# A scheduler that knows how long things take: traced durations, overlaps and a hold on TensorE in a four-layer transformer kernel

## The chip, the cores and the metric

The kernel runs on one core of a Trainium2 chip. The metric is the time of the whole kernel on the device, in microseconds, from the first to the last instruction of that core. A core has five engines that run their own instruction streams and wait for each other through semaphores: TensorE (PE; its weight loads are listed as PEld) for matrix products, VectorE (DVE), ScalarE (ACT), GpSimd (POOL), and SyncE (SP), which issues transfers here.

## The reference

Four layers over x of 2048 tokens by 512: attention, feed-forward, attention, feed-forward, with the same weights for both attentions and for both feed-forwards. Each has a layer norm before it and adds to x; the feed-forward has a second layer norm of its own.

```python
def _A_ref(x, wqkv, wo):                  # attention, 32 heads of 16
    qkv = (x @ wqkv) ...                  # q, k, v: (1, 32, 2048, 16)
    scores = jnp.einsum("bhqd,bhkd->bhqk", q, k) * scale
    p = _softmax(scores, axis=-1)
    o = jnp.einsum("bhqk,bhkd->bhqd", p, v)
    return o... @ wo
def _B_ref(x, w1, b1, w2, b2):            # feed-forward, 1376 wide
    y = _layernorm(x, axis=-1)
    h = _gelu(jnp.einsum("bsd,df->bsf", y, w1) + b1)
    return jnp.einsum("bsf,fd->bsd", h, w2) + b2

x = A_x
x = x + _A_ref(_layernorm(x, axis=-1), A_wqkv, A_wo)
x = x + _B_ref(_layernorm(x, axis=-1), B_w1, B_b1, B_w2, B_b2)
x = x + _A_ref(_layernorm(x, axis=-1), A_wqkv, A_wo)
x = x + _B_ref(_layernorm(x, axis=-1), B_w1, B_b1, B_w2, B_b2)
```

With 32 heads of 16, each attention has 32 x 2048 x 2048 scores, so exponentials[...]. Cut into tiles of 128 keys by 512 queries that is 4096 tiles for both attentions.

## The kernel before

The kernel is a Python program that works like a list scheduler. It keeps a model of the five engines: when each is free (`free`), when each value was written (`t1`) and read. Jobs hand in tasks with a priority (lower goes first), a modelled duration, and what they read and write. The scheduler picks the task that can start earliest, appends its instructions to its engine's stream, and moves the model's clock on. What the chip gets is only the order on each engine and the semaphores; the modelled times are not in it. But they decide the order, and some decisions on the work itself.

The model: an operation starts when its engine is free and what it depends on is ready.

```python
LAT_SAME = 0.07
LAT_CROSS = 0.13
LAT_PE = 0.22
PE_SWITCH = 0.107          # TensorE changes its tiling
...
    def ready(self, eng, reads, writes, same_ok=()):
        ...                # d: an operation that this one depends on
                x = d.t1 + (LAT_SAME if d.eng == eng else LAT_PE if d.eng == "pe" else LAT_CROSS)
        ...
        return t
    def op(self, eng, fn, reads=(), writes=(), same_ok=(), dur=0.3, lat=None):
        op.t0 = max(self.free[eng], self.ready(eng, reads, writes, same_ok))
        ...
        elif eng == "pe":
            how, tile = lat or ("full", 0)
            if how != self.tiling:
                op.t0 = max(op.t0, self.drain + PE_SWITCH)
            ...
        else:
            op.t1 = op.t0 + dur
            self.free[eng] = op.t1
```

The choice on an engine: of the tasks that are ready when it is free, the one with the lowest priority number; if none is ready, the one that will be ready first.

```python
    def best(self, e):
        f = self.P.free[e]
        lim = f + self.LOOK[e]
        for t in lst:
            r = self.task_ready(t)
            if r <= lim:
                k = (t.prio, t.seq)
                if bk is None or k < bk:
                    b, bk = t, k
                    br = r
            else:
                ...        # late: the one that will be ready first
```

The work of attention. TensorE makes scores for 3 and 2 tiles in turn (PSUM banks 0 to 2 and 3 to 4); ScalarE takes the exponential of a group in one instruction:

```python
            yield Task("pe", 0.0, ops)                                        # L1204: scores
            S_.submit(Task("act", 1e-5 * gi, [I(lambda e, ...: e.activation(
                out=self.PT[:, pt:pt + n, :], in_=self.ps[:, b0:b0 + n, :],
                func=ACTF.Exp, scale=EXPS), ..., 0.089 + 0.4267 * n)]), ...)  # L1189
```

A tile of certain key blocks can go to VectorE instead. There the bits of the exponential are made by an addition with rounding to 16-bit integers (L1281), then three shifted copies (L1312), which together with four scaled versions of V approximate the exponential. Such a tile needs four products with V (L1373) in place of one. Whether a tile goes there is decided by the model:

```python
    def take_d(self, hps):
        if ... self.dload > 1 or P.free["dve"] - S_.now > 1.3 \
               or sum(o[4] for t in S_.pend["dve"] for o in t.ops) > DBACK:   # 2.0
            return None
        ...                # up to 4 - (tiles of the group) are attached to each group of scores
    # L1281                                                        modelled 0.66
    e.tensor_scalar(out=self.dp[...], in0=self.ps[:, b, :], scalar1=BITS0, ..., op0=ALU.add)
    # L1312, N = 1024 for two tiles, three times                   modelled 0.1 + 0.26e-3 * N
    e.tensor_scalar(out=self.dp[:, v, 0:N], in0=self.dp[:, u, 0:N], scalar1=float(SHIFT[k]), ..., op0=ALU.add)
```

The scores have priority 0.0 and an attached VectorE tile's scores -0.5. A VectorE tile that is scored on its own has 0.5, a product of probabilities with V 1.0, and output projection, feed-forward and the next layer's q, k and v have 0.95 to 2.2. While TensorE has a gap of over 0.2 us in the model, `fill_pe` puts products into it whose result nobody uses (L1114, L1117)[...]. GELU (L1530, L1531) runs on ScalarE between the exponentials and needs two table loads each time.

Of the kernel before, what the change touches and what calls it, by code (L numbers as in the profile page):

```python
# [13 lines left out]
ACTF = mybir.ActivationFunctionType  # L14
ALU = mybir.AluOpType
# [4 lines left out]
LAT_SAME = 0.07  # L20
LAT_CROSS = 0.13
LAT_PE = 0.22
# [40 lines left out]
class Prog:  # L63
# [14 lines left out]
    def ready(self, eng, reads, writes, same_ok=()):  # L78
        t = 0.0
        lw, rd = self.last_writer, self.readers  # L80
        for r in reads:
            d = lw.get(r)
            if d is not None and not (d.eng == eng and r in same_ok):
                x = d.t1 + (LAT_SAME if d.eng == eng else LAT_PE if d.eng == "pe" else LAT_CROSS)
                if x > t:
                    t = x
        for w in writes:
            d = lw.get(w)
            if d is not None and not (d.eng == eng and w in same_ok):
                x = d.t1 + (LAT_SAME if d.eng == eng else LAT_PE if d.eng == "pe" else LAT_CROSS)  # L90
                if x > t:
                    t = x
            q = rd.get(w)
            if q:
                for d in q.values():
                    if not (d.eng == eng and w in same_ok):
                        x = d.t1 + (LAT_SAME if d.eng == eng else LAT_PE if d.eng == "pe" else LAT_CROSS)
                        if x > t:
                            t = x
        return t  # L100

    def op(self, eng, fn, reads=(), writes=(), same_ok=(), dur=0.3, lat=None):
# [10 lines left out]
        if eng == "sp":  # L113
            self.free[eng] = op.t0 + dur
            op.t1 = op.t0 + dur + (2.0 if lat is None else lat)
# [4 lines that stand above are left out]
                self.tiling, self.tiles = how, {}  # L120
            op.t0 = max(op.t0, self.tiles.get(tile, 0.0))
            op.t1 = op.t0 + dur
            self.tiles[tile] = op.t1
            self.drain = max(self.drain, op.t1)
            self.work.append((op.t0, op.t1, 1.0 if how == "full" else 0.25))
            self.free[eng] = op.t0 + min(dur, PE_ISSUE)
        else:
            op.t1 = op.t0 + dur
            self.free[eng] = op.t1
# [134 lines left out]
class Sched:  # L264
# [44 lines left out]
    def _step(self, gen, prio, val):  # L309
        while True:  # L310
# [24 lines left out]
            if kind == "ready":  # L335
                r = self.P.ready(req[1], req[2], ()) - 0.3
                if r <= self.now:
                    continue
                self.seq += 1
                heapq.heappush(self.timers, (r, self.seq, lambda: self._step(gen, prio, None)))  # L340
                return
# [31 lines left out]
    def best(self, e):  # L373
        lst = self.pend[e]
        if not lst:
# [3 lines that stand above are left out]
        b = None  # L379
        bk = None  # L380
        late = None
        lk = None
        for t in lst:
            r = self.task_ready(t)
            if r <= lim:
                k = (t.prio, t.seq)
                if bk is None or k < bk:
                    b, bk = t, k
                    br = r
            else:  # L390
                k = (r, t.prio, t.seq)
                if lk is None or k < lk:
                    late, lk = t, k
        if b is not None:
            return (max(f, br), b)
        return (lk[0], late)

# [28 lines left out]

FILL_GAP = 0.2
# [24 lines left out]
class Builder:  # L452
# [314 lines left out]
    def ln_group(self, tiles, slot, prio, eps1, eps0):  # L767

        for i, tt in enumerate(tiles):
            c = 4 * slot + i  # L770
            s = yield ("get", "st")
            yield Task("dve", prio, [I(lambda e, s=s, tt=tt: e.bn_stats(out=self.st[:, s, :], in_=self.xres[:, tt, :]), [("x", tt)], [("st", s)], 0.65)])
            yield Task("dve", prio, [I(lambda e, s=s, c=c: e.bn_aggr(out=self.mv[:, c, :], in_=self.st[:, s, :]), [("st", s)], [("mv", c)], 0.18)])
            self.S_.release("st", s)
# [5 lines left out]
        yield Task("pool", prio, [I(lambda e: e.tensor_scalar(out=rs, in0=var, scalar1=eps1, scalar2=eps0, op0=ALU.mult, op1=ALU.add), [("mv", c0 + i) for i in range(n)], [R], 0.25)])  # L780
        yield Task("pool", prio, [I(lambda e: e.tensor_tensor(out=rs, in0=rs, in1=self.cneg[:, 0:n], op=ALU.pow), [R, ("cneg",)], [R], 0.45 + 0.1 * n)])

    def ln_apply(self, tt, slot, i, dst, dres, prio):
        c = 4 * slot + i
        return Task("dve", prio, [I(lambda e: e.tensor_scalar(out=dst, in0=self.xres[:, tt, :], scalar1=self.mv[:, c, 0:1], scalar2=self.rs[:, c:c + 1], op0=ALU.subtract, op1=ALU.mult),
                                    [("x", tt), ("mv", c), ("rs", slot)], [dres], 0.39)])
# [19 lines left out]
    def job_qkv_tile(self, L, tt, slot, i, left, prio, what):  # L806
# [74 lines left out]
        yield Task(eng, prio, [I(lambda e: e.tensor_tensor(out=sq, in0=v4, in1=v4, op=ALU.mult), [("qk", qs, k) for k in range(k0, k1)], SR, 0.12 + 0.0085 * N if eng == "dve" else 1.15)])  # L881
# [26 lines left out]
    def bound_rows(self, qs, ns, RN, prio, eng="pool"):  # L908
# [7 lines left out]
        yield Task(eng, prio, [I(lambda e: e.tensor_tensor(out=a, in0=x, in1=y, op=ALU.mult), RN + [("qy", ns)], [RA], 0.35 if eng == "pool" else 0.17)])  # L916
        yield Task(eng, prio, [I(lambda e: e.tensor_tensor(out=c, in0=a, in1=y, op=ALU.mult), [RA, ("qy", ns)], [RC], 0.3 if eng == "pool" else 0.17)])
        yield Task(eng, prio, [I(lambda e: e.tensor_scalar(out=c, in0=c, scalar1=-0.5, scalar2=1.5, op0=ALU.mult, op1=ALU.add), [RC], [RC], 0.28 if eng == "pool" else 0.17)])
        yield Task(eng, prio, [I(lambda e: e.tensor_tensor(out=a, in0=a, in1=c, op=ALU.mult), [RA, RC], [RA], 0.3 if eng == "pool" else 0.17)])
        yield Task(eng, prio, [I(lambda e: e.tensor_scalar(out=pads(self.qks(qs)[:, 0, :])[:, :, 16:17], in0=a.rearrange("p (n o) -> p n o", o=1), scalar1=-MARG, scalar2=0.0, op0=ALU.mult, op1=ALU.add),  # L920
                                    [RA], [QQ], 0.4 if eng == "pool" else 0.17)])
# [120 lines left out]
    def job_qt(self, sg, s):  # L1042
# [8 lines left out]
                                  [RS, ("scl", k), ("qbias",)], [("qt", q)], 0.39)])  # L1051
# [8 lines left out]
    def job_vs(self, sg, i, kbs):  # L1060
# [5 lines left out]
                                   [("V", hg, kb) for kb in kbs], [("vs", q, i + k2) for k2 in range(n)], 0.27 + 0.167 * n, [("vs", q, i + k2) for k2 in range(n)] if k > 1 else []) for k in (1, 2, 3)])  # L1066
# [58 lines left out]
    def flow_scores(self):  # L1125
# [11 lines left out]
        while True:  # L1137
# [45 lines left out]
            if len(ops[0]) > 1:  # L1183
# [6 lines left out]
                                                [("ps", b) for b in banks], [("pt", pt + k) for k in range(n)], 0.089 + 0.4267 * n)]),  # L1190
# [86 lines left out]
    def d_load(self, d):  # L1277
# [4 lines left out]
                                           [("ps", b)], [("dp", u, w)] + self.dres(u), 0.66)]),  # L1282
# [21 lines left out]
    def job_d(self, bt):  # L1304
# [4 lines left out]
        for k in range(1, len(SHIFT)):  # L1309
# [3 lines left out]
                                     [("dp", u, w) for w in range(n)], [("dp", v, w) for w in range(n)] + self.dres(v), 0.1 + 0.26e-3 * N)])  # L1313
# [82 lines left out]
    def job_segend(self, sg):  # L1396
# [6 lines left out]
        yield Task("dve", 0.3, [I(lambda e: e.transpose(self.accT[:, a, 0:W], self.ps[:, ACCB, 0:W]), [("ps", ACCB)], [RA], 0.15 + 0.53 * W / 512)])  # L1403
# [21 lines left out]
        if nparts == 2:  # L1425
# [4 lines left out]
            yield Task("act", -1.0, [I(lambda e: e.activation(out=dw, in_=dw, func=ACTF.Exp, scale=EXPS), [RW], [RW], 0.2)])  # L1430
            yield Task("pool", 1.2, [I(lambda e: e.tensor_tensor(out=M, in0=M, in1=dw.unsqueeze(2).broadcast_to([128, 16, 16]), op=ALU.mult), [RW, RO], [RO], 0.75),
                                     I(lambda e: e.tensor_tensor(out=den, in0=den, in1=dw, op=ALU.mult), [RW, RD], [RD], 0.2),
                                     I(lambda e: e.tensor_tensor(out=T[:, :, 16], in0=T[:, :, 16], in1=den, op=ALU.add), [RD, RA], [RA], 0.2),
# [7 lines left out]
        yield Task("dve", 1.2, [I(lambda e: e.tensor_tensor(out=ob[:, :, 0:16], in0=T[:, :, 0:16], in1=rv.unsqueeze(2).broadcast_to([128, nb, 16]), op=ALU.mult), [RA, ("rv", a)], [("ob", o)], 0.15 + 0.26 * W / 512)])  # L1441
# [66 lines left out]
    def job_ffn(self, L, qc):  # L1508
# [8 lines left out]
        for fc in range(NFC):  # L1517
# [7 lines left out]
                                               [("ps", b), ("b1c",)], self.hres(fc * W // 512), 0.1 + 0.52 * W / 512, [("h", fc * W // 1024)])]),  # L1525
# [4 lines left out]
        yield Task("act", -1.0, [I(lambda e: e.activation(out=self.gv[:, 0:nf * W], in_=hv[:, 0:nf * W], func=ACTF.Gelu_apprx_tanh), HR, HR, 1.5 + 0.427 * nf * W / 512),  # L1530
                                I(lambda e: e.activation(out=self.g10[0:self.FLAST, 0:W], in_=hv[0:self.FLAST, nf * W:(nf + 1) * W], func=ACTF.Gelu_apprx_tanh), HR, [("g10",)], 0.5 + 1.3)])  # L1531
# [23 lines left out]
    def job_tail(self, L, qc):  # L1555
# [14 lines left out]
        yield Task("act", pr, [I(lambda e: e.activation(out=self.kmx[:, 2:3], in_=self.kmx[:, 0:1], func=ACTF.Gelu_apprx_tanh), [("kmx", 0)], [("kmx", 2)], 1.4)])  # L1570
# [14 lines left out]
        for fc in range(NFC):  # L1585
# [5 lines left out]
                                          [("ps", b), ("b1c",)], [("gt", fc)] + (HR if fc == 0 else [("g10",)] if fc == nf else []), 0.16 + 0.52 * W / 512)]),  # L1591
# [122 lines left out]
```

## Time and profile before

| | before |
|---|---|
| median of 3 runs | 1661.06 us (1657.99 to 1662.54) |
| span of the profiled run | 1661.8 us |
| busy: PE, DVE, ACT | 1608.0, 1452.7, 1582.4 us |
| score tiles through ScalarE, through VectorE | 3270, 826 |
| mean granted TensorE clock | 0.994 of full |

The profile's groups name a line of the kernel, an engine, an operation, what it writes and reads with its shape, how often it ran, its total and mean duration, and the idle time of the engine before it with what ended most of that. The waits name who waited, for whom, how long in total, how often, and the longest. Durations of two consecutive instructions on ScalarE or VectorE can overlap, so a busy share is one thing, and how often an instruction can start another. On the time line each row is an instruction or a merged run of the same kind: start, length, engine, line, and in brackets the idle time before it and who ended it.

### The profile page before, as it was taken

To read this page: it belongs to the slowest core of one execution; us is meant where nothing else is said; L and a number is where in the kernel's file an instruction comes from. 1 tells how busy PE (TensorE), PEld (TensorE's weight loads), DVE (VectorE), ACT (ScalarE), POOL (GpSimd) and SP (SyncE) were. 2 spreads that over 40 slices of the span, in tenths; PEclk is the share of its full clock that TensorE was granted. 3 is DMA by queue.
4 is the path that set the end of the run, shared out by engine and by line. 5 is a ranking of instruction groups with operands and counts; after the bars stand their busy time and mean duration, and the time that the engine had idled before them with its cause. 6 is when DMAs were issued, how large, how long until landed. Compare 5 with 4: busy or idle time off the path is not lost.

```text
span 1661.8 us, 42068 instructions
## 1 busy us (share of the span) xinstructions
PE 1608.0 (97%) x17575; PEld 529.0 (32%) x17575; DVE 1452.7 (87%) x3146; ACT 1582.4 (95%) x1400; POOL 376.1 (23%) x575
## 2 busy tenths in 40 slices
PE   8999999999999999999999999999999999999998
PEld 5223322222222232222232323322232232344444
DVE  7789998888899898998989789999898969899893
ACT  4899999999999999999999999999999999999996
POOL 4345331111210112111121125511111111232220
PEclk9999999999999999999999999999999999899999
DMA  6562100202111121102362321000000000000000
GB/s 170 103 125 62 27 8 8 42 19 61 56 23 42 26 52 53 33 26 58 95 94 57 59 64 42 18 18 8 20 5 11 17 16 5 5 9 20 22 7 14
DMA packets 181243, 66.43 MB, mean 40 GB/s; under 512 B 160859, under 2 KB 175424, under 8 KB 181056
## 3 DMA queue, kind: packets, MB, share of 16 engines
q1 hardware_dynamic: 181056, 63.75, 17.3%
q8 instruction: 141, 2.31, 0.6%
q14 instruction: 46, 0.38, 0.1%
HBM read 19.96 MB, written 15.30 MB: 21 GB/s over the span
## 4 chain that ended last, share of the span: by engine, by line
PE 65%; ACT 27%; DVE 6%; issue 1%; DMA 1%; POOL 0%; POOLq 0%; SPq 0%; DVEq 0%
ACT PT L1189 25%; PE ps L1204 24%; PE ps L1373 19%; PE ps L840 5%; PE ps L1500 4%; PE ps L1538 4%; PE ps L1114 4%; PE ps L1467 3%; DVE dp L1281 2%; DVE dp L1312 2%; ACT h L1530 1%; PE ps L1117 1%; PE ps L953 1%; DMA xnT<-xn 0%; ACT L1189 0%
## 5 line engine op out<-in xcount | busy, mean ns | idle before, releaser
L1189 ACT ACTIVATE PT<-ps 128x1024 bf16<-128x1024 f32 (+1 forms) x1321 | 1506.4, 1259 | 49.5 <-PE ps L1204 43.1
L1204 PE MATMUL ps<-QT,KT 32*128 32x512 bf16 (+1 forms) x4608 | 681.8, 359 | 39.0 <-ACT PT L1189 16.9
L1281 DVE TENSOR_SCALAR dp<-ps 128x512 uint16<-128x512 f32 x826 | 558.2, 684 | 117.0 <-PE ps L1204 108.0
L1312 DVE TENSOR_SCALAR dp<-dp 128x1024 uint16<-128x1024 uint16 (+1 forms) x1257 | 488.8, 431 | 11.1 <-PE ps L1373 6.7
L1373 PE MATMUL ps<-PT,V 128*17 128x512 bf16 (+1 forms) x3672 | 486.7, 360 | 0.3 <-ACT PT L1189 0.3
L1065 POOL TENSOR_SCALAR vs<-V 128x340 bf16<-128x340 bf16 (+3 forms) x240 | 238.5, 995 | 875.3 <-PE ps L1373 851.0
L1373 PE MATMUL ps<-dp,vs 128*17 128x512 bf16 (+1 forms) x2808 | 420.7, 357 | 0.0
L1204 PEld LDWEIGHTS ps<-QT,KT 32*128 32x128 bf16 x4608 | 176.4, 91 | 568.3 <-issue 170.7
L1373 PE MATMUL ps<-dp,V 128*17 128x512 bf16 (+1 forms) x936 | 204.6, 359 | 2.7 <-DVE accT L1403 2.5
L1114 PE MATMUL ps<-wqkv,zw 128*32 128x256 bf16 x3792 | 182.0, 277 | 0.4 <-DVE dp L1281 0.4
L1373 PEld LDWEIGHTS ps<-PT,V 128*17 128x17 bf16 x3672 | 116.4, 88 | 119.4 <-issue 107.5
L1373 PEld LDWEIGHTS ps<-dp,vs 128*17 128x17 bf16 x2808 | 106.2, 89 | 113.6 <-issue 94.2
L1114 PEld LDWEIGHTS ps<-wqkv,zw 128*32 128x32 bf16 x3792 | 97.1, 96 | 67.1 <-issue 50.0
L1500 PE MATMUL ps<-yT,wf 128*128 128x512 bf16 (+3 forms) x396 | 101.7, 360 | 0.3 <-DVE dp L1281 0.3
L840 PE MATMUL ps<-wqkv,xnT 128*128 128x512 bf16 x336 | 96.1, 389 | 4.3 <-DMA xnT<-xn 3.4
L1403 DVE STREAM_TRANSPOSE accT<-ps 128x512 f32<-128x512 f32 (+1 forms) x88 | 58.0, 659 | 13.7 <-PE ps L1373 12.7
L1467 PE MATMUL ps<-wo,OT 128*128 128x512 bf16 x240 | 67.2, 383 | 0.0
L1373 PEld LDWEIGHTS ps<-dp,V 128*17 128x17 bf16 x936 | 50.5, 89 | 48.1 <-issue 26.7
L1524 DVE TENSOR_SCALAR h<-ps,b1c 128x512 bf16<-128x512 f32 (+2 forms) x88 | 61.9, 704 | 3.6 <-PE ps L1500 2.9
L1443 DVE STREAM_TRANSPOSE OT<-ob 128x512 bf16<-128x512 bf16 (+1 forms) x72 | 46.0, 638 | 0.2
L1500 PEld LDWEIGHTS ps<-yT,wf 128*128 128x128 bf16 (+1 forms) x396 | 28.1, 99 | 54.2 <-issue 26.9
L1538 PE MATMUL ps<-wf,h 128*128 128x512 bf16 x160 | 44.9, 383 | 0.1
(171 smaller groups left out, 794.7 us busy)
## 6 DMA issues: line engine op xcount, KB each, us to landing
wf<-in_B_w_dram SPq DMA_DIRECT2D x90, 128.0 KB, 2.6
q_scr<-qk SPq DMA_DIRECT2D x22, 256.0 KB, 2.0
k_scr<-qk SPq DMA_DIRECT2D x12, 256.0 KB, 2.1
out_dram<-xres SPq DMA_DIRECT2D x16, 128.0 KB, 1.7
v_scr<-vst SPq DMA_DIRECT2D x12, 136.0 KB, 1.7
V<-v_scr SPq DMA_DIRECT2D x8, 204.0 KB, 4.7
wqkv<-in_A_wqkv_dram SPq DMA_DIRECT2D x3, 512.0 KB, 3.9
q_scr<-h SPq DMA_DIRECT2D x6, 256.0 KB, 3.6
```

Source lines behind the costliest of these rows:

```text
L840: yield Task("pe", prio, [I(lambda e, c=c: e.matmul(self.ps[:, b, :], lhsT=xnT[:, c, :], rhs=self.wqkv[:, c, which * 512:which * 512 + 512 ...
L1065: yield Task("pool", 0.8, [I(lambda e, k=k: e.tensor_scalar(out=self.vs[:, q, k - 1, i:i + n, :], in0=src, scalar1=WSHIFT[k], scalar2=None ...
L1114: P.op("pe", lambda e, p=p: e.matmul(self.ps[p:p + 32, b, 0:w], lhsT=self.zw[:, 0:32], rhs=rhs[:, 0:w], start=st, stop=st, skip_group_chec ...
L1189: S_.submit(Task("act", 1e-5 * gi, [I(lambda e, pt=pt, n=n, b0=b0: e.activation(out=self.PT[:, pt:pt + n, :], in_=self.ps[:, b0:b0 + n, :] ...
L1204: return [I(lambda e, kb=kb, i=i: e.matmul(self.ps[:, b, i * W:(i + 1) * W], lhsT=self.KT[32 * hp:32 * hp + 32, hg, kb * 128:(kb + 1) * 12 ...
L1281: self.S_.submit(Task("dve", 0.0, [I(lambda e: e.tensor_scalar(out=self.dp[:, u, w * 512:(w + 1) * 512], in0=self.ps[:, b, :], scalar1=BIT ...
L1312: yield Task("dve", pr, [I(lambda e, k=k, v=v: e.tensor_scalar(out=self.dp[:, v, 0:N], in0=self.dp[:, u, 0:N], scalar1=float(SHIFT[k]), sc ...
L1373: ops.append((i, I(lambda e, hp=hp, v=v, ap=ap[:, i * W:(i + 1) * W], first=first and i == 0, W=W: e.matmul(self.ps[32 * hp:32 * hp + 17, ...
L1467: yield Task("pe", pr, [I(lambda e, hg=hg, i=i, b=b: e.matmul(self.ps[:, b, :], lhsT=self.OT[:, hg, i * 128:(i + 1) * 128], rhs=self.wo[:, ...
L1500: yield Task("pe", pr, [I(lambda e, c=c: e.matmul(self.ps[0:M, b, off:off + W], lhsT=self.w1(fc, c), rhs=self.yT[:, c, 0:W], start=(c == 0 ...
L1524: S_.submit(Task("dve", pr - 0.7, [I(lambda e, fc=fc, M=M, b=b: e.tensor_scalar(out=hv[0:M, fc * W:(fc + 1) * W], in0=self.ps[0:M, b, 0:W] ...
L1538: yield Task("pe", pr, [I(lambda e, fc=fc, i=i, b=b: e.matmul(self.ps[:, b, :], lhsT=self.gt(fc, i, W), rhs=self.w2(L, fc), start=(fc == 0 ...
```

## The change

The scheduler's model gets the durations that a trace of the kernel shows, in place of rounder ones; it lets an instruction on ScalarE, VectorE or GpSimd start before the one ahead of it has ended, by a fixed overlap; and the delay from a dependency to the start now belongs to the engine that waits, with an extra for results of TensorE. Beside that comes a rule for TensorE: a task with priority over 0 (products with V, projections, feed-forward, a VectorE tile on its own) is passed over if the next scores will be ready within 1 us and TensorE would drain too late for them. The purpose is that the order fits the engines as they are, and that ScalarE doesn't wait for scores. The computation is the same.

```diff
-LAT_SAME = 0.07
-LAT_CROSS = 0.13
-LAT_PE = 0.22
+LATENCY = {"act": 0.036, "dve": 0.036, "pool": 0.086, "pe": 0.057, "sp": 0.06}
+LAT_PE = 0.174
+OVERLAP = {"act": 0.127, "dve": 0.08, "pool": 0.05}
 PE_SWITCH = 0.107
...
-                x = d.t1 + (LAT_SAME if d.eng == eng else LAT_PE if d.eng == "pe" else LAT_CROSS)
+                x = d.t1 + LAT_PE if d.eng == "pe" else d.t1
...
-        return t
+        return t + LATENCY[eng] if t else 0.0
...
             op.t1 = op.t0 + dur
-            self.free[eng] = op.t1
+            self.free[eng] = op.t0 + (max(0.02, dur - OVERLAP[eng]) if lat is None else lat)
...
+        due = self.scores_due(f, lim) if e == "pe" else None
         for t in lst:
             r = self.task_ready(t)
             if r <= lim:
+                if due is not None and t.prio > 0.0 and self.drained(t, max(f, r)) + PE_SWITCH > due:
+                    continue
...
+    def scores_due(self, f, lim):
+        first = None
+        for t in self.pend["pe"]:
+            if t.prio == 0.0:
+                r = self.task_ready(t)
+                if r > lim and (first is None or r < first):
+                    first = r
+        if first is None or first - f > HOLD_REACH:
+            return None
+        act = self.P.free["act"] + sum(max(0.02, o[4] - OVERLAP["act"]) for t in self.pend["act"] for o in t.ops)
+        return max(first, act - HOLD_LEAD) + HOLD_LATE
+
+    def drained(self, task, t):
+        ...                # when TensorE would have done this task, its tiling switch included
...
+HOLD_REACH = 1.0
+HOLD_LEAD = 0.45
+HOLD_LATE = 0.4
...                        # exponential of n tiles, L1189
- ... 0.089 + 0.4267 * n)]),
+ ... 0.174 + 0.428 * n)]),
...                        # VectorE's tiles, L1281 and L1312
- ... 0.66)]),
+ ... 0.682)]),
- ... 0.1 + 0.26e-3 * N)])
+ ... 0.151 + 0.2605e-3 * N)])
...                        # bias before GELU, L1524
- ... 0.1 + 0.52 * W / 512, ...
+ ... 0.2 + 0.54 * W / 512, ...
...                        # GELU, L1530 and L1531: durations, and when ScalarE is free again
- ... 1.5 + 0.427 * nf * W / 512), ... 0.5 + 1.3)])
+ ... 1.5 + 0.427 * nf * W / 512, (), 1.313 + 0.2 + 0.427 * nf * W / 512), ... 0.2 + 0.427 * W / 512, (), 0.2 + 1.32 + 0.427 * W / 512)])
```

Some twenty more durations of small operations (layer norms, norms of queries and keys, scaled copies of V, transposes) change in the same way, most by 0.01 to 0.1 us.

## The prediction

> **What bounds the kernel now.** I read the page's busy times first, then the groups by form, then who waits for whom, then the time line round one wait.
>
> ```profile
> PE 1608.0 (97%) x17575; PEld 529.0 (32%) x17575; DVE 1452.7 (87%) x3146; ACT 1582.4 (95%) x1400; POOL 376.1 (23%) x575
> ```
>
> Three engines look full. ScalarE (ACT) is the one that is: TensorE (PE) holds filler products among its 1608 us, and a busy PE is not PE at its peak. The groups by form:
>
> ```profile
> L1189 ACT ACTIVATE PT<-ps 128x1536 bf16<-128x1536 f32 x628 | 931.0, 1483 | 29.6 <-PE ps L1204 23.7
> L1189 ACT ACTIVATE PT<-ps 128x1024 bf16<-128x1024 f32 x693 | 727.5, 1057 | 19.9 <-PE ps L1204 19.3
> ...
> L1281 DVE TENSOR_SCALAR dp<-ps 128x512 uint16<-128x512 f32 x826 | 558.2, 684 | 117.0 <-PE ps L1204 108.0
> L1312 DVE TENSOR_SCALAR dp<-dp 128x1024 uint16<-128x1024 uint16 x1221 | 479.8, 434 | 11.0 <-PE ps L1373 6.7 <-DVE xres L1469 0.3
> ...
> L1114 PE MATMUL ps<-wqkv,zw 128*32 128x256 bf16 x3792 | 182.0, 277 | 0.4 <-DVE dp L1281 0.4
> ```
>
> The 4096 score tiles of 512 columns are split: 628 x 3 + 693 x 2 = 3270 go through ScalarE's exponential, 826 through VectorE (one read from PSUM, and three shifted copies for each pair of tiles). So each tile that moves from ScalarE to VectorE shortens ScalarE's queue. L1114 is filler. The waits:
>
> ```profile
> DVE dp L1281 <- PE ps L1204: 108.0, 210, 3.5
> ...
> PEld ps L1204 <- ACT PT L1189: 62.1, 165, 0.9
> ...
> ACT PT L1189 <- PE ps L1204: 43.1, 102, 4.1
> ```
>
> ScalarE waits for scores 43.1 us in 102 places, VectorE 108 us. One such place on the time line:
>
> ```profile
> 277.48 0.60 PE L1204 MATMUL ps<-QT,KT 32*128 32x512 bf16 x3
> 278.01 0.55 PEld L1467 LDWEIGHTS ps<-wo,OT 128*128 128x128 bf16 x4 [0.42 <-issue]
> 278.02 1.04 PE L1467 MATMUL ps<-wo,OT 128*128 128x512 bf16 x4
> 278.12 0.69 DVE L1281 TENSOR_SCALAR dp<-ps 128x512 uint16<-128x512 f32 x1 [0.20 <-PE ps L1204]
> 278.98 0.11 PEld L1204 LDWEIGHTS ps<-QT,KT 32*128 32x128 bf16 x4 [0.42 <-PE ps L1467]
> 278.99 0.60 PE L1204 MATMUL ps<-QT,KT 32*128 32x512 bf16 x4
> 279.48 1.45 ACT L1189 ACTIVATE PT<-ps 128x1536 bf16<-128x1536 f32 x1 [0.27 <-PE ps L1204]
> ```
>
> Four output-projection products went between two sets of scores; the second set came late and ScalarE stood 0.27 us. This is what the hold is aimed at.
>
> **What the Trainium skill says.** "ScalarE: Activation LUTs", under "What ACT_TABLE_LOAD costs", gives an ACTIVATE with immediate operands 186 ns + 0.833 ns per element, and says that neighbours overlap by about 93 ns. The trace agrees in form: means of 1483 and 1057 ns (the rule gives 1466 and 1039), and consecutive starts lie a median 1.331 us apart after a 3-tile exponential and 0.903 (lower quartile) after a 2-tile one, so they overlap by some 0.10 to 0.13. "TensorEngine Tiling (Array Packing)", under "Key Properties", says that changing the tiling mode drains TensorE: above, the scores of 277.48 start 0.53 us after the first of two full products (276.95), which stream for 0.43, so a switch costs about 0.10, as the kernel's constant (0.107, unchanged) has it. "VectorE: DVE Perf Modes", under "Why PSUM operands drop a tier", explains why L1281 takes 684 ns for 512 elements from PSUM, while L1312 takes 434 for 1024 in SBUF. "TensorE: Matmul & The Clock Gate", under "What's actually happening", says that an idle array falls to half clock: this trace has a mean of 0.994, and 0.86 in 1400 to 1450 us.
>
> **The change, part by part.** No instruction gets another shape; the order on each engine, and the split between ScalarE and VectorE, come out of the model, and the model changes.
>
> 1. *ScalarE's durations.* Old model: 0.089 + 0.4267n, so 1.369 and 0.942 for n = 3 and 2: 2.311 us for five tiles. New: 0.174 + 0.428n - 0.127, so 1.331 and 0.903: 2.234. The trace has 1.331 + 0.903 = 2.234. The old order was laid out for a ScalarE 3.4% slower than it is, so TensorE took on other products in time that wasn't there. The whole floor: 628 x 1.331 + 693 x 0.903 = 1462 us, or 0.447 per tile; the remaining 199 us are GELU with its table loads (about 60), start and tail (28 us before the first exponential, 22 after the last), and gaps. Adding up how much each start is late against 1.331 or 0.903 gives 88 us from first to last exponential, some 80 of it in gaps over 0.1 us, a gap being here a delay with or without a named wait.
>
> 2. *VectorE's durations.* Old: 0.66 for L1281, 0.1 + 0.26 x 1.024 = 0.366 for L1312; a pair of tiles costs 2 x 0.66 + 3 x 0.366 = 2.42 us. New: 0.682 - 0.08 = 0.602 and 0.151 + 0.267 - 0.08 = 0.338; a pair costs 2.22. The trace has medians of 0.608 and 0.336 between starts: 2.22. So VectorE gets 8% cheaper in the model, ScalarE only 3.4%. Tiles are given to VectorE as long as its modelled backlog is under 1.3 us (and 2.0 us pending), so it should get more of them. How many? Old model: 826 tiles x 1.21 + about 490 for other work = 1490, which is 90% of 1661. New: 1.10 per tile; other work is 461 us (546 measured less 0.08 for each of 1063). If the model again fills 90%: 1.10n + 461 = 0.9T, with T = 1641 - 0.447(n - 826) (20 us of gaps already gone): n = 896. If instead only the measured share is kept (durations less 0.08: 499 + 441 + 461 = 1401 us, 84%): n = 835. I take the middle, **865**: 39 tiles x 0.447 = **-17 us** on ScalarE. The pending limit still adds up full durations, which grew, and the hold keeps PSUM readers waiting; hence not the upper end.
>
> 3. *The hold.* Products with priority over 0 wait when they would drain later than the next scores are due plus 0.4 us. That forbids the long delays (277 to 279 above), not those of 0.2 us. With part 1 I let 20 to 25 of the 80 us go: **-20 us**. The first 60 us (14 us of score waits while the first keys arrive) are DMA and product latency, and stay.
>
> 4. *What it costs.* Each tile moved to VectorE needs four products with V instead of one: 39 x 3 x 0.216 / 4 = 6 us of TensorE, off the path as long as there is filler to give up. From 100 to 1640 us the starts on TensorE divide into 590 us of scores, 483 of products with V, 301 of full products, 165 of filler and the gaps before what follows it. So 165 us are spare, and a time 37 us shorter takes them to about 120. Enough on average, not in each stretch.
>
> Sum: 1661 - 17 - 20 = **1624 us**.
>
> **Rivals.** *TensorE becomes the bound.* Holding makes it stand idle, and what is held (feed-forward, projections, next layer's keys) comes due at the layer's end near 850 to 960 us, where ScalarE already loses 6.7 us. For it: 97% busy, and only a tenth spare. Against: that tenth is filler. Then the hold's gain is given back: about 1645 to 1660. *VectorE takes many more tiles.* For it: 108 us of waits for scores and the 90% estimate above; against: L1281 waits for TensorE, which serves it together with ScalarE's scores. Then 890 to 900 tiles, 30 us, and with the gaps: 1600 to 1610. *Only the model changes, the chip hardly follows.* ScalarE is 95% busy and every order that keeps it fed is nearly as good; the limits tuned to the old model (1.3, 2.0, 0.3 ahead) fit the new one less well: 1640 to 1660. *More half clock.* Held stretches could let the array idle: a stretch like 1400 to 1450, with 3.9 us of waits, costs some 4 us each time.
>
> **Range and chances.** The good end is part 2's upper count with 35 us of gaps recovered: 1661 - 31 - 35 = 1595, so 1592 to be safe. The bad end is no gain with a little noise: 1656. 2% faster is 1627.8, just above the sum, so it is little better than even: faster 0.54, same 0.41, slower 0.05, the last for a jam on TensorE that the spare 165 us don't cover.
>
> **What would show it.** Right: L1281 rises from 826 to about 865 and L1189's tiles fall from 3270 to about 3230; ACT's wait for L1204 falls from 43 to about 25, DVE's from 108 to under 90; filler L1114 falls from 3792 to near 2800; L1189's share of the chain rises over 25%. Wrong in part 2: L1281 stays within 10 of 826. Wrong in part 3: ACT's wait for L1204 stays over 38, or PE's waits on ACT grow by as much as ACT's fall. The whole is wrong if ScalarE's busy share falls under 94%.

## The result, and the profile after

| | before | after |
|---|---|---|
| median | 1660.42 us (4 runs, 1657.99 to 1662.54) | 1641.84 us (4 runs, 1640.56 to 1643.21) |
| ratio, 95% interval | | 0.9887 (0.9871 to 0.9903) |
| tiles through ScalarE, VectorE | 3270, 826 | 3227, 869 |
| ScalarE's wait for scores | 43.1 us | 43.0 us |
| filler products L1114, now L1150 | 3792 | 2928 |

The change takes 18.6 us off, 1.1%. In the changed file attention and feed-forward stand 36 lines lower: L1240 makes the scores, L1225 is the exponential, L1317 and L1348 are VectorE's tiles, L1409 the products with V, L1566 GELU. The page's busy times:

```profile
PE 1555.6 (95%) x16682; PEld 504.4 (31%) x16833; DVE 1481.7 (90%) x3255; ACT 1562.2 (95%) x1383; POOL 380.0 (23%) x575
```

ScalarE has 20.2 us less to do (1582.4 before), VectorE 29 us more, TensorE 52 us less, most of that filler. The groups by form:

```profile
L1225 ACT ACTIVATE PT<-ps 128x1536 bf16<-128x1536 f32 x620 | 915.0, 1476 | 35.2 <-PE ps L1240 29.2
L1225 ACT ACTIVATE PT<-ps 128x1024 bf16<-128x1024 f32 x683 | 712.8, 1051 | 14.2 <-PE ps L1240 13.8
...
L1317 DVE TENSOR_SCALAR dp<-ps 128x512 uint16<-128x512 f32 x869 | 583.6, 679 | 76.8 <-PE ps L1240 72.9
L1348 DVE TENSOR_SCALAR dp<-dp 128x1024 uint16<-128x1024 uint16 x1284 | 505.8, 434 | 6.7 <-PE ps L1409 1.8
...
L1150 PE MATMUL ps<-wqkv,zw 128*32 128x256 bf16 x2928 | 142.7, 277 | 0.3 <-DVE accT L1439 0.3
```

620 x 3 + 683 x 2 = 3226 and one exponential of a single tile make 3227 tiles: 43 have moved to VectorE, and the mean of none of these shapes moved by more than 7 ns. At the 0.447 us per tile of the prediction 43 tiles are 19.2 us, which is the whole gain. The last column of the two L1225 rows adds to 43.0 us of waiting for scores: what ScalarE waits for in all hasn't moved. The list of waits has the same number, and one that grew. Before:

```profile
PEld ps L1204 <- DVE dp L1281: 41.2, 95, 1.1
...
PE ps L1204 <- DVE dp L1281: 8.7, 22, 0.8
```

and after:

```profile
DVE dp L1317 <- PE ps L1240: 72.9, 110, 2.4
PEld ps L1240 <- DVE dp L1317: 70.2, 155, 1.9
PEld ps L1240 <- ACT PT L1225: 50.9, 144, 0.7
...
ACT PT L1225 <- PE ps L1240: 43.0, 94, 2.7
...
PE ps L1240 <- DVE dp L1317: 14.9, 35, 1.6
```

VectorE waits for scores 35 us less. TensorE now waits longer for VectorE to read a PSUM bank: 70.2 us at the weight loads and 14.9 at the products, 85.1 together, where the kernel before had 41.2 + 8.7 = 49.9. The chain that ended last shows it too. Of before, by engine:

```profile
PE 65%; ACT 27%; DVE 6%; issue 1%; DMA 1%; POOL 0%; POOLq 0%; SPq 0%; DVEq 0%
```

and of after, by engine and by line:

```profile
PE 49%; DVE 24%; ACT 23%; issue 3%; DMA 1%; POOL 1%; DVEq 0%; SPq 0%
ACT PT L1225 21%; PE ps L1240 19%; PE ps L1409 14%; DVE dp L1317 9%; DVE dp L1348 7%; PE ps L1574 4%; PE ps L1536 4%; PE ps L876 3%; PE ps L1503 3%; PE ps L1150 2%; DVE accT L1439 1%; DVE OT L1479 1%; ACT h L1566 1%; DVE QT L1086 1%; DVE ob L1477 1%
```

In the kernel before, L1189 had 25% of the chain. Read alone, VectorE's share of 6% turned into 24% says that VectorE is the new bound, and that its banks hold TensorE up. Experiment 8 tests that.

### The profile page after: what moved, and what is told of

It reads as the page before. It is cut to its first block, busy times and chain, and to the rows that moved or that the text cites. A ratio compares the mean times of both kernels' runs of the same rounds, so it can differ in the third digit from the quotient of the medians.

```text
span 1641.4 us, 40475 instructions
## 1 busy us (share of the span) xinstructions
PE 1555.6 (95%) x16682; PEld 504.4 (31%) x16833; DVE 1481.7 (90%) x3255; ACT 1562.2 (95%) x1383; POOL 380.0 (23%) x575
## 4 chain that ended last, share of the span: by engine, by line
PE 49%; DVE 24%; ACT 23%; issue 3%; DMA 1%; POOL 1%; DVEq 0%; SPq 0%
ACT PT L1225 21%; PE ps L1240 19%; PE ps L1409 14%; DVE dp L1317 9%; DVE dp L1348 7%; PE ps L1574 4%; PE ps L1536 4%; PE ps L876 3%; PE ps L1503 3%; PE ps L1150 2%; DVE accT L1439 1%; DVE OT L1479 1%; ACT h L1566 1%; DVE QT L1086 1%; DVE ob L1477 1%
## 5 line engine op out<-in xcount | busy, mean ns | idle before, releaser
L1225 ACT ACTIVATE PT<-ps 128x1024 bf16<-128x1024 f32 (+1 forms) x1304 | 1486.0, 1253 | 49.4 <-PE ps L1240 43.0
L1240 PE MATMUL ps<-QT,KT 32*128 32x512 bf16 (+1 forms) x4608 | 685.6, 359 | 44.0 <-DVE dp L1317 14.9
L1317 DVE TENSOR_SCALAR dp<-ps 128x512 uint16<-128x512 f32 x869 | 583.6, 679 | 76.8 <-PE ps L1240 72.9
L1348 DVE TENSOR_SCALAR dp<-dp 128x1024 uint16<-128x1024 uint16 (+1 forms) x1323 | 515.0, 430 | 6.9 <-PE ps L1409 1.8
L1409 PE MATMUL ps<-PT,V 128*17 128x512 bf16 (+1 forms) x3624 | 489.0, 359 | 0.5 <-DVE accT L1439 0.4
L1409 PE MATMUL ps<-dp,vs 128*17 128x512 bf16 (+1 forms) x2952 | 435.8, 358 | 1.2 <-DVE dp L1348 0.9
L1240 PEld LDWEIGHTS ps<-QT,KT 32*128 32x128 bf16 x4608 | 178.0, 91 | 574.8 <-issue 151.6
L1409 PE MATMUL ps<-dp,V 128*17 128x512 bf16 (+1 forms) x984 | 209.8, 360 | 1.7 <-DVE accT L1439 0.9
L1409 PEld LDWEIGHTS ps<-PT,V 128*17 128x17 bf16 x3624 | 116.2, 88 | 115.1 <-issue 103.6
L1409 PEld LDWEIGHTS ps<-dp,vs 128*17 128x17 bf16 x2952 | 109.7, 88 | 127.2 <-issue 108.2
L1150 PE MATMUL ps<-wqkv,zw 128*32 128x256 bf16 x2928 | 142.7, 277 | 0.3 <-DVE accT L1439 0.3
L1536 PE MATMUL ps<-yT,wf 128*128 128x512 bf16 (+3 forms) x356 | 93.7, 357 | 7.4 <-issue 4.1
L876 PE MATMUL ps<-wqkv,xnT 128*128 128x512 bf16 x299 | 84.5, 383 | 9.7 <-issue 3.2
L1150 PEld LDWEIGHTS ps<-wqkv,zw 128*32 128x32 bf16 x2928 | 73.3, 96 | 58.7 <-issue 41.6
L1503 PE MATMUL ps<-wo,OT 128*128 128x512 bf16 x209 | 60.8, 382 | 5.0 <-issue 3.7
L1409 PEld LDWEIGHTS ps<-dp,V 128*17 128x17 bf16 x984 | 51.2, 88 | 45.7 <-issue 25.4
```

The source lines that it names most:

```text
L876: yield Task("pe", prio, [I(lambda e, c=c: e.matmul(self.ps[:, b, :], lhsT=xnT[:, c, :], rhs=self.wqkv[:, c, which * 512:which * 512 + 512 ...
L1150: P.op("pe", lambda e, p=p: e.matmul(self.ps[p:p + 32, b, 0:w], lhsT=self.zw[:, 0:32], rhs=rhs[:, 0:w], start=st, stop=st, skip_group_chec ...
L1225: S_.submit(Task("act", 1e-5 * gi, [I(lambda e, pt=pt, n=n, b0=b0: e.activation(out=self.PT[:, pt:pt + n, :], in_=self.ps[:, b0:b0 + n, :] ...
L1240: return [I(lambda e, kb=kb, i=i: e.matmul(self.ps[:, b, i * W:(i + 1) * W], lhsT=self.KT[32 * hp:32 * hp + 32, hg, kb * 128:(kb + 1) * 12 ...
L1317: self.S_.submit(Task("dve", 0.0, [I(lambda e: e.tensor_scalar(out=self.dp[:, u, w * 512:(w + 1) * 512], in0=self.ps[:, b, :], scalar1=BIT ...
L1348: yield Task("dve", pr, [I(lambda e, k=k, v=v: e.tensor_scalar(out=self.dp[:, v, 0:N], in0=self.dp[:, u, 0:N], scalar1=float(SHIFT[k]), sc ...
```

## Experiments

After the result three theories stood. **Share**: the gain is the 43 tiles, and the new order is worth nothing beside them. **Hold**: the hold gains, and something else of the change gives it back. **Banks**: the hold's gain went into TensorE's longer waits for VectorE's banks. A fourth came with the first results, **the layer's end**: what comes late in the feed-forward delays the second attention's first scores.

For each kernel the table has the median, and the ratio to the kernel before on the same chip (its medians there: 1659.9 for 1 to 4, 1661.7 for 5 to 8, 1661.1 for 9 to 12).

| | VectorE tiles | us | ratio (95%) | ACT waits for scores |
|---|---|---|---|---|
| before | 826 | 1660.4 | 1 | 43.1 |
| the change | 869 | 1641.8 | 0.9887 (0.9871 to 0.9903) | 43.0 |
| 1 no hold | 875 | 1657.0 | 0.9982 (0.9956 to 1.0009) | 54.9 |
| 2 hold on the old model | 830 | 1671.3 | 1.0060 (1.0039 to 1.0081) | 48.5 |
| 3 VectorE's durations alone | 878 | 1668.0 | 1.0037 (1.0019 to 1.0055) | 59.7 |
| 4 ScalarE's durations alone | 833 | 1685.0 | 1.0153 (1.0106 to 1.0200) | 66.5 |
| 5 limit of the hold 0.3 | 863 | 1650.7 | 0.9941 (0.9923 to 0.9959) | 64.4 |
| 6 limit of the hold 0.5 | 882 | 1689.2 | 1.0160 (1.0141 to 1.0180) | 101.3 |
| 7 tiles held down | 820 | 1668.7 | 1.0045 (1.0024 to 1.0066) | 43.0 |
| 8 banks free earlier | 838 | 1658.1 | 0.9985 (0.9968 to 1.0002) | 43.2 |
| 9 limit 0.5, feed-forward early | 871 | 1650.5 | 0.9939 (0.9919 to 0.9959) | 50.8 |
| 10 no hold, feed-forward early | 881 | 1656.4 | 0.9972 (0.9951 to 0.9994) | 56.9 |
| 11 limit 0.3, feed-forward early | 861 | 1648.9 | 0.9921 (0.9894 to 0.9948) | 45.2 |
| 12 combined | 856 | 1645.6 | 0.9904 (0.9871 to 0.9938) | 38.6 |

### 1. The new model without the hold

```diff
-        due = self.scores_due(f, lim) if e == "pe" else None
+        due = None
```

> The changed kernel without the hold rule (the new durations, overlaps and delays stay); VectorE gets 875 score tiles. Theory S (the gain is the share that moves from ScalarE to VectorE, 0.447 us per tile, and the order hardly matters): 1660 - 49 x 0.447 = 1638 us, between 1634 and 1645, and ScalarE's wait for scores stays at 40 to 50 us. Theory H (the hold made the gain): back to 1653 or more.

Measured: 1656.97 us, 15 above the change, with 6 tiles more on VectorE. ScalarE's wait:

```profile
ACT PT L1225 <- PE ps L1240: 54.9, 118, 5.2
```

So on the new model the hold does what it is for: 54.9 us in 118 places become 43.0 in 94. But the kernel before had 43.1. The new model had first put 12 us of waits there, which the hold took away again. The longest waits here, 5.2 and 3.3 us, lie at 827 to 846 us, where the second attention begins. With 49 tiles more than before, the share by itself would have given 1634 to 1645 us: that theory falls, as far as it says that the order hardly matters.

### 2. The hold on the old model

```diff
+        due = self.scores_due(f, lim) if e == "pe" else None
...
+                if due is not None and t.prio > 0.0 and self.drained(t, max(f, r)) + PE_SWITCH > due:
+                    continue
...                # scores_due without the overlap, drained as in the change
```

> The kernel before with only the hold rule added, old durations and delays; VectorE gets 830 tiles. Theory S: 1660 - 4 x 0.447 = 1658, between 1654 and 1662. Theory H: 1642 to 1648, with ScalarE's wait for scores under 30 us.

Measured: 1671.29 us, 11 slower than before and above what either theory expected; ScalarE's wait is 48.5. The hold isn't good by itself: added to the old model it costs 11 us, taken out of the changed kernel (1) it costs 15. That it needs a model whose times are near the chip's would explain both, but isn't shown.

### 3. VectorE's durations and overlap alone

```diff
+OVERLAP = {"act": 0.0, "dve": 0.08, "pool": 0.0}
...
-            self.free[eng] = op.t1
+            self.free[eng] = op.t0 + (max(0.02, dur - OVERLAP[eng]) if lat is None or not OVERLAP[eng] else lat)
...
- ... 0.66)]),                    # VectorE's tile
+ ... 0.682)]),
- ... 0.1 + 0.26e-3 * N)])        # shifted copies
+ ... 0.151 + 0.2605e-3 * N)])
...                               # and VectorE's small operations
```

> The kernel before with only VectorE's durations and overlap of 0.08 taken from the change, no hold, old delays; VectorE gets 878 tiles. Theory S: 1660 - 52 x 0.447 = 1637, between 1633 and 1645. Theory H, and a theory that ScalarE's corrected durations made the gain: 1653 to 1661.

Measured: 1668.01 us with 878 tiles on VectorE, 52 more than before, so VectorE's durations are what moves the tiles. 52 x 0.447 = 23 us left ScalarE's queue, and the time rose by 8, where 1633 to 1661 was expected:

```profile
PEld ps L1205 <- DVE dp L1282: 72.5, 140, 2.1
ACT PT L1190 <- PE ps L1205: 59.7, 130, 3.3
```

(here L1205 makes the scores, L1190 is the exponential, L1282 VectorE's tile). ScalarE's wait went from 43.1 to 59.7. Adding up how late each exponential starts after the one before it, against 1.331 or 0.903 us, gives 111 us where the kernel before has 88. A tile that moves is worth 0.447 us only if the order still brings ScalarE its scores in time.

### 4. ScalarE's durations and overlap alone

```diff
+OVERLAP = {"act": 0.127, "dve": 0.0, "pool": 0.0}
...                               # self.free as in 3
- ... 0.089 + 0.4267 * n)]),
+ ... 0.174 + 0.428 * n)]),
...                               # and GELU, with when ScalarE is free again
```

> The kernel before with only ScalarE's durations and overlap of 0.127 taken from the change, no hold, old delays; VectorE gets 833 tiles. Theory S: 1660 - 7 x 0.447 = 1657, between 1653 and 1662. The theory that ScalarE's corrected durations made the gain: 1640 to 1646.

Measured: 1684.97 us, 25 slower than before and far above both expectations; the wait for scores is 66.5 us. 15.4 of them are one stop from 850 us on, where the second attention's scores come late; the other 51 are still more than before. The right durations for ScalarE by themselves don't take the gaps away. What the new delays from a dependency to the start do wasn't tried by itself.

### 5 and 6. The hold's limit, 0.3 and 0.5 us

```diff
-HOLD_LATE = 0.4
+HOLD_LATE = 0.3       # 5
+HOLD_LATE = 0.5       # 6
```

> The changed kernel with the hold a little stricter: scores may be 0.3 us late instead of 0.4. VectorE gets 863 tiles. If the hold works by what it forbids, waits of ScalarE over 0.4 us get still fewer and the time stays at 1638 to 1650. If its 15 us are the luck of one order out of many, the time can be anywhere from 1640 to 1665.

> The changed kernel with the hold a little looser, 0.5 instead of 0.4; VectorE gets 882 tiles. If the hold works by what it forbids: between the change and the kernel without a hold, 1642 to 1657. If it is luck of the order, it can lie outside, above 1660.

Measured: 1650.7 and 1689.2 us on the two sides of the change's 1641.84. 6 lies where "luck of the order" had put it, and no smooth optimum lies behind such numbers. The time line of ScalarE with limit 0.5 has the reason. Each row is a start, a length, and in brackets how long the engine had stood:

```profile
759.03 4.47 ACT L1566 ACTIVATE h<-h 128x5120 bf16<-128x5120 bf16 x1
...
828.42 3.28 ACT L1225 ACTIVATE PT<-ps 128x1024 bf16<-128x1024 f32 x3 [0.35 <-PE ps L1240]
881.14 9.14 ACT L1225 ACTIVATE PT<-ps 128x1536 bf16<-128x1536 f32 x8 [49.44 <-PE ps L1240]
```

The first attention has ended, the second hasn't got its first scores, and ScalarE stands 49.4 us. All engines in that stretch:

```profile
862.06 0.23 DVE L1057 TENSOR_SCALAR scl<-ps,onesm 128x8 f32<-128x8 f32 x1 [0.19 <-PE ps L1056]
...
874.97 5.25 SPq L1109 DMA_TRANSPOSE KT<-k_scr  x3
...
880.65 0.60 PE L1240 MATMUL ps<-QT,KT 32*128 32x512 bf16 x5
```

L1057 is the scale of queries and keys. This one needs the norms of the first 12 of the second attention's 16 blocks of keys, so three of the four units of the first feed-forward (the fourth unit's GELU comes later, in 6 at 898 us); then the last keys are loaded and the first scores are made. In each of ten traces L1057 comes 90 to 103 us after the GELU of the third feed-forward unit, and the first attention has its last exponentials at about 827 to 850:

| | GELU of the third unit | L1057 | stops over 2 us at the change of layer |
|---|---|---|---|
| the change | 726.8 | 823.0 | none |
| before | 729.6 | 827.5 | none |
| 1 | 732.9 | 829.2 | 3.3 and 5.2 us |
| 5 | 751.4 | 846.2 | 16.4 us |
| 4 | 755.0 | 857.5 | 15.4 us |
| 6 | 759.0 | 862.1 | 49.4 us |
| 9 | 725.2 | 815.7 | none |
| 10 | 724.8 | 816.6 | none |
| 11 | 730.5 | 826.4 | none |
| 12 | 727.4 | 820.5 | none |

The third unit's feed-forward work has priority 1.6, behind the products with V at 1.0. When it gets its turn on TensorE depends on how many free places the order leaves. In 6 ScalarE has 1491 of its tiles ahead of that GELU, in the change 1433: the order alone makes it 58 x 0.447 = 26 of the 32 us later. In 5 it is 1463 tiles, so 13 of 25 us. The profiled run of 5 had a mean granted clock of 0.96 up to there, where the change had 0.99, so a part of the stop of 16.4 us may be that run's clock and not the order.

### 7. The change with the old number of tiles

```diff
- ... P.free["dve"] - S_.now > 1.3 ...
+ ... P.free["dve"] - S_.now > 0.6 ...
-DBACK = 2.0
+DBACK = 0.923076923076923
```

> The changed kernel with the limits on VectorE's backlog lowered (0.6 us and 0.92 us pending) so that it gets 820 tiles, as before the change. Theory that moved tiles are the gain once the hold keeps order: 1642 + 49 x 0.447 = 1664, less what fewer waits for VectorE's bank give back, so 1652 to 1666. Theory that order alone is the gain: 1637 to 1645.

Measured: 820 tiles, 1668.65 us, a little above what was expected; ScalarE's wait 43.0, as in the change. Against the change it is 26.8 us slower, and 49 tiles x 0.447 are 21.9 of that. (The last section puts the other 5 down to the clock.) So the new model and the hold with the old share bring nothing over the kernel before; they make it possible to keep the larger share at the same waits, which 3 couldn't. Of the three theories, share is right on where the gain comes from, and wrong that the order doesn't matter.

### 8. VectorE's banks free earlier

A tile goes to VectorE only if its bank is free in the model by the time that TensorE comes to it plus 0.1 us.

```diff
-        soon = lambda b: P.ready("pe", (), [("ps", b)]) <= max(S_.now, P.free["pe"]) + 0.1
+        soon = lambda b: P.ready("pe", (), [("ps", b)]) <= max(S_.now, P.free["pe"]) + -0.1
```

> The changed kernel in which a tile goes to VectorE only if its PSUM bank has been free for 0.1 us in the model when TensorE comes to it (before: it may become free up to 0.1 us later); VectorE gets 838 tiles. Theory that TensorE stands before banks that VectorE returns late, and ScalarE with it: TensorE's waits for VectorE's reading of scores (85 us in the change) fall under 40, ScalarE's waits fall by 10 or more, and the time is 1642 + 31 x 0.447 - 10 to 15 = 1641 to 1646. If those waits hit nothing: about 1656.

Measured: 838 tiles, 1658.06 us.

```profile
ACT PT L1225 <- PE ps L1240: 43.2, 99, 2.7
...
PEld ps L1240 <- DVE dp L1317: 35.4, 82, 1.3
```

TensorE's waits for VectorE's bank are halved (40 us with those at the products, instead of 85), and ScalarE's wait is what it was. 31 tiles fewer than the change cost 31 x 0.447 = 14 us, 1656 in all. The theory of the banks falls: ScalarE doesn't wait less when TensorE waits less for VectorE, so most of those waits seem to lie where TensorE had time to spare. VectorE's share of the chain is 26% here, with half the waits, so that share didn't measure them.

### 9, 10 and 11. The feed-forward earlier, with limits 0.5, none and 0.3

```diff
-        return 0.95 if (L, qc) == (1, self.NC - 1) else 1.6 if (L, qc) == (1, self.NC - 2) else 2.2
+        return 0.95 if (L, qc) == (1, self.NC - 1) else 1.05 if (L, qc) == (1, self.NC - 2) else 1.6 if L == 1 else 2.2
```

with `HOLD_LATE = 0.5` in 9, `due = None` in 10, and `HOLD_LATE = 0.3` in 11.

> The hold of 0.5 us again, with the feed-forward work of the first layer raised in priority (1.6 for the first two units instead of 2.2, 1.05 for the third instead of 1.6); VectorE gets 871 tiles. Theory J (the long stop of ScalarE near 830 us comes because the chain from the third unit's GELU to the second attention's first scores ends too late): the third GELU comes before 735 us, the stop of 49.6 us is gone, and the time is 1689 - 45 to 50, so 1638 to 1648. If the stop has another cause: over 1665.

> No hold, with the same raised priorities; VectorE gets 881 tiles. If the hold's 15 us were only that it happened to avoid stops at the layer change: 1636 to 1643, level with the change. If the hold also takes away waits of 0.4 to 1 us all along: 1645 to 1653.

> The hold of 0.3 us with the same raised priorities; VectorE gets 861 tiles. Theory J: the stop of 16.5 us is gone: 1650 - 16 = 1634, between 1630 and 1642. If a strict hold starves TensorE so that its other work comes late elsewhere: 1645 or more.

Measured: 1650.53, 1656.42 and 1648.88 us. ScalarE in 9, where 6 had its stop:

```profile
725.16 4.47 ACT L1566 ACTIVATE h<-h 128x5120 bf16<-128x5120 bf16 x1
...
807.71 34.15 ACT L1225 ACTIVATE PT<-ps 128x1536 bf16<-128x1536 f32 x30 [0.21 <-PE ps L1240]
842.05 8.55 ACT L1225 ACTIVATE PT<-ps 128x1536 bf16<-128x1536 f32 x7 [0.20 <-PE ps L1240]
```

The GELU is 34 us earlier than in 6, the exponentials run through, and the time falls by 39 us. That confirms the layer's end as the cause of 6. It doesn't for 5: 11 has no such stop, and its median is only 1.8 us lower, where 16 was expected. All three medians lie above the range that was expected of them, by 2.5, 3.4 and 6.9 us; the last section looks for that in the clock. With the stop gone in all three, the hold's limit has an orderly effect on ScalarE's wait: 56.9 us without a hold, 50.8 at 0.5, 45.2 at 0.3, each from one trace, at mean clocks of 0.989, 0.988 and 0.987. (The change, with 0.4 and the old priorities, has 43.0.) So the hold works along the way as well, not just by keeping clear of the stop.

### 12. Combined

Limit 0.3, banks at +0.05, the third unit of the first feed-forward at 1.0 and the first two at 1.6; the second feed-forward gets 1.6 as well, instead of 2.2:

```diff
-HOLD_LATE = 0.4
+HOLD_LATE = 0.3
- ... max(S_.now, P.free["pe"]) + 0.1
+ ... max(S_.now, P.free["pe"]) + 0.05
- ... else 1.6 if (L, qc) == (1, self.NC - 2) else 2.2
+ ... else 1.0 if (L, qc) == (1, self.NC - 2) else 1.6
```

> A version meant to beat both: hold of 0.3 us, priorities 1.6, 1.0 for the third unit and 1.6 in the second feed-forward, and a tile goes to VectorE only if its bank is free by at most 0.05 us after TensorE comes to it (0.1 in the change); VectorE gets 856 tiles. Without long stops and with fewer waits for banks: 1660 - 30 x 0.447 - 10 = 1637, between 1628 and 1642. If ScalarE's share alone counts: 1647.

Measured: 1645.63 us (1638.15 to 1651.0 in 4 runs), 13 tiles fewer than the change. ScalarE's wait is the lowest of all:

```profile
ACT PT L1225 <- PE ps L1240: 38.6, 59, 4.4
```

and still the median isn't below the change's, and above the 1628 to 1642 that was expected; the intervals of the two ratios overlap. Its best run is 4 us faster than the change's median, and its others are slower at a lower clock. That is the subject of the last section.

## Why the prediction was right or wrong

The prediction said 1624 us in 1592 to 1656; the time is 1641.84. The range holds it, the size of the gain was half of what the sum said, and "faster by over 2%" at 0.54 was more likely in it than what came.

- **What bounds the kernel**: right. ScalarE's queue is what the time follows: 43 tiles less are 19.2 us, the time fell by 18.6. 7 takes the tiles back and gives the gain back.
- **Part 1, ScalarE's durations**: the numbers are right (consecutive starts as modelled), the conclusion isn't. "TensorE took on other products in time that wasn't there" would mean that right durations shorten the waits. In 4 they made them longer, 43.1 to 66.5; leaving out the stop at the change of layer, to 51. With the whole new model and no hold (1) it is 54.9.
- **Part 2, VectorE's durations**: right in the mechanism. 865 tiles were expected, 869 came; 17 us expected, 19 are there. That it came so near is in part luck: 865 was the middle of 835 and 896, and with other limits of the hold (1, 5, 6) it is 863 to 882. 3 shows that it is VectorE's durations that do it. What the step took for granted, that the moved tiles cost nothing elsewhere, holds only with the hold: in 3, tiles worth 23 us moved, and the time rose by 8 with later scores.
- **Part 3, the hold**: this is the step that failed. "With part 1 I let 20 to 25 of the 80 us go: -20 us." ScalarE's wait for scores stayed at 43.0 and the lateness of its starts went from 88 to 85.5 us, so the term measured 0 to 3 us against the kernel before. The mechanism is real: 1 without it is 15 us slower, and the waits fall from 54.9 to 43.0. But the prediction took the gaps of the old order as what the hold would find. The order with the new durations and the larger share had 12 us more of waits, and those are what the hold took back. The two long waits at the change of layer in 1 are 8.4 us, but they aren't the whole of the 12: 10, also without a hold, has no such wait and 56.9 us in all.
- **Part 4, TensorE's spare time**: right. Filler was to fall to near 2800 products and fell to 2928, for a time that fell half as far.
- **What was to show it**: VectorE's wait under 90 (72.9) and ScalarE's busy share over 94% (95%) came. L1189's share of the chain was to rise over 25% and fell to 21%: more of the chain went through VectorE instead. As 8 shows, that share says little on the bound here, so the check was a bad one. "ACT's wait for L1204 stays over 38" was named as what would show part 3 wrong, and it did.
- **The rivals**: *TensorE becomes the bound* at the layer's end isn't in the change. 6, one step of 0.1 us away, does lose 49.4 us there, but not for want of TensorE: from 832 to 880 us it ran 159 filler products (19.7 us). What came late was the order of the feed-forward, which the prediction didn't have. *VectorE takes many more tiles*: no. *Only the model changes, the chip hardly follows* has the right range of time (1640 to 1660) and the wrong reason: a share of tiles moved, and the model did decide it. *More half clock*: not in the change, whose runs have about 10 us of it against 17 before, but in its neighbours.

What stays open: 5, 6 and 9 to 12 show that a schedule next to this one can be 4 to 47 us away, so a part of the change's lead over them is its having met neither the stop nor a low clock. The change itself was timed in 4 runs. And why the new durations, which fit the trace, give later scores without the hold (1, 3, 4) was not found; only that they do. In 1 and 3 the 49 and 52 tiles more on VectorE, with four products each, may be a part of it; 4 has only 7 more, so for part 1 the cause stays open.

## What to carry to other kernels

Where a scheduler's model decides how work is split between two engines, correcting its durations first changes the split: work out that term by itself. Here two readings of the same model gave 835 and 896 tiles, and 869 came. A gain that a rule is to bring must be taken from the gaps of the order that the other parts of the change produce, not from those in the profile of before. And before a constant of such a scheduler is judged by the total time, look for a single long stop at a change of stage: one can outweigh everything that the constant does along the way.

## What the runs showed of the hardware

The time of one and the same kernel followed the time that TensorE spent at half clock, though ScalarE is the engine that sets the end. In the trace of the change the granted clock is 1.00 in most stretches and 0.50 in some. If a mean clock of 1 - x means that the share 2x of the run was at half clock, 96 runs of the kernel before give 1655.5 us + 0.39 us for each microsecond at half clock (correlation 0.97). Of other kernels: 0.31 in 5, 0.41 in 1, 0.37 in 8, 0.36 in 3. One kernel, 5, has runs from 1644.17 us at a clock of 0.994 to 1662.47 at 0.979. The Trainium skill, "TensorE: Matmul & The Clock Gate", "What's actually happening", has an idle array fall to half clock; the trace of the change agrees in this place:

```profile
164.38 0.10 PEld L1240 LDWEIGHTS ps<-QT,KT 32*128 32x128 bf16 x3 [1.15 <-DVE dp L1317]
...
166.04 0.10 PEld L1240 LDWEIGHTS ps<-QT,KT 32*128 32x128 bf16 x1 [0.97 <-DVE dp L1317]
166.05 0.60 PE L1240 MATMUL ps<-QT,KT 32*128 32x512 bf16 x1 [0.68 <-DVE dp L1317]
...
166.58 0.59 PE L1409 MATMUL ps<-PT,V 128*17 128x512 bf16 x1
...
167.54 1.04 PE L1240 MATMUL ps<-QT,KT 32*128 32x512 bf16 x6
168.25 2.37 ACT L1225 ACTIVATE PT<-ps 128x1536 bf16<-128x1536 f32 x2 [2.35 <-PE ps L1240]
```

TensorE stood twice for about a microsecond, then took 0.59 to 0.60 us for products that took 0.38 at 164.99 us, and ScalarE stood 2.35 us. The granted clock was 1.00 from 163 to 165 us and 0.50 from 166 to 170. The page speaks of an idle window of about 3.4 us; here no single stretch is over 1.15, and TensorE was busy for 1.30 of the 3 us from 163 to 166, so the clock fell with no idle stretch of that length. The time at half clock isn't the same in each run of one order, so it is scatter that an order is more or less open to: the medians at half clock are 17 us before, 10 in the change, and 33, 33, 43 and 41 in 9 to 12.

That is where the gain of 12 went. Taking 0.38 us for each microsecond at half clock off gives estimates for full clock: 1655.7 before, 1637.4 for the change, 1634.1 for 11 and 1629.6 for 12. And less 0.4466 us for each of ScalarE's tiles, what is left is 195 before, 196 for the change, and 195 in 7 and 8: the same four times, with shares from 820 to 869 tiles. It is 205 without a hold (10), 200 with a limit of 0.5 (9), 189 with 0.3 (11) and 183 in 12; with the old priorities it is 210 without a hold (1), 196 with 0.4 (the change) and 192 with 0.3 (5), so little of the stop in 5's trace shows in its runs. So a stricter hold does seem to shorten the path at full clock, and against the change its runs lose 9 to 12 us of that at the clock: (33 to 43, less 10) x 0.38. These are fits over few runs of each kernel, so the split between order and clock is an estimate. Whether more of the filler products in the held places would keep the clock up, and so keep both, was not tried.
